# Partial sums of two recurrences formed by TensorE up to step 12 instead of step 7, with new instruction orders

## The chip, the cores and the metric

The kernel runs on one NeuronCore of one Trainium2 chip. The metric is the device time of one execution in microseconds, the median of several executions. A core has five engines with a queue each: TensorE (PE, with its weight loads as PEld), VectorE (DVE), ScalarE (ACT), GpSimd (POOL) and SyncE (SP). SP only issues DMAs here. The engines work through their queues strictly in the order written, and wait for each other at semaphores.

## The reference: what is computed

Two kinds of layer alternate, A, B, A, B, each with a layer norm before it and its result added to x (2048 tokens of 448 numbers).

```python
def _A_ref(x, mem0, Wq, Wk, Wv, Wo, seg_len):      # 16 heads of 256, 8 memory rows, segments of 32
    ...
    for s in range(n_seg):                          # 64 segments, one after the other
        h = jnp.concatenate([mem, xs], axis=1)      # 8 memory rows + 32 rows of x
        q, k, v = ...                               # h times Wq, Wk, Wv
        scores = jnp.einsum('bhqe,bhke->bhqk', q, k) * scale
        p = _softmax(jnp.where(mask, scores, -1e9))
        o = jnp.einsum('bhte,hed->btd', jnp.einsum('bhqk,bhke->bhqe', p, v), Wo)
        mem = o[:, :M, :].copy()                    # the next segment's memory
        outs.append(o[:, M:, :])
```

Layer B is a gated product: relu(x Wg) * (x Wu), times Wd. What makes it hard is `mem`: the 8 memory rows of segment s+1 are made from segment s, so layer A is a recurrence of 64 steps, and there are two of them (the first and the third layer). Only the 8 memory rows have to go through the recurrence. The other rows of a segment can be computed later, in tiles of 128 tokens.

## The kernel before, in words

**Folded weights.** At the start, Wq and Wk are folded into one matrix per head (tile `A`) and Wv and Wo into another (tile `Bsb`), so that scores are (h A) h^T and the output is P h Bsb.

**Steps.** The function `chain(step)` advances both recurrences by one segment. The second runs `LAG` = 7 steps behind the first. So steps 0 to 6 hold one recurrence, steps 7 to 62 both, and steps 63 to 69 the second alone. Columns 0 to 7 of the transposed memory `mT` belong to the first, 8 to 15 to the second. From step 7 on columns 16 to 31 carry 16 **riders**: rows of already finished tokens that are not part of a recurrence (their attention is computed along with it). One step is, on TensorE:

1. `U`, line 1268: mT times A, 112 matmuls into four banks, copied to `Usb` by ACT and DVE (line 1274).
2. Line 1444: turns `Usb` into `uTm`; then the scores, line 1467; softmax on DVE and ACT (lines 1477 to 1484); line 1507 turns the probabilities; line 1537 and 1541 multiply with the rows `HR`; the result is copied to `YTm`.
3. The **product**, line 1307: `YTm` times `Bsb`, 56 chunks. TensorE works on four column groups at once, so that the result lies in four partial sums in partitions 0-31, 32-63, 64-95 and 96-127 of one bank, and has to be added across partitions.
4. The **sum** of the four, and its transposition into the new `mT` by the column matmuls (line 1334 or 1350), which the next step's `U` needs.

The sum is made in one of two ways.

- Steps 0 to 6 (`step < LAG`, line 1312): the product is made in two halves of 256 and 192 columns. ACT copies each half of the bank as bf16 into `Hi` (line 1314), DVE writes bank minus Hi into `Lo` (line 1315), and eight column matmuls (line 1334, two for each of four blocks) with the selection matrix `Sel16` add the four parts, Hi and Lo, and transpose in one go. Two further matmuls (line 1341, the **row matmuls**) form the sum untransposed in 16 partitions, and a copy puts it into `Ohi` (line 1355).
- Steps 7 and later: ACT copies part 0 (line 1322), DVE adds parts 1, 2 and 3 one after the other (1324 twice, 1325) into `Ohi`, GpSimd or DVE doubles a piece (`twice`, line 1205), and four column matmuls (line 1350) transpose. In step 7 this is done in two halves (`step < SPLIT`), from step 8 on at once.

From `Ohi`, four DMAs write the new memory rows into `HR` (lines 1364 and 1365), and two more bring riders' rows to `Tsb` (line 1371).

**Where Hi and Lo lie.** They share their memory with `UR`. The riders' part of `Usb` is turned by DMA into `UR`, first for half v = 0, then for v = 1 (`turn_riders`, line 1415), and copied from there to `uTr` by ACT or DVE after each. The riders' scores (1467), softmax (1493 to 1501) and products (1534) run beside the chain.

**What fills the time between.** TensorE has other work: tiles of the attention (1626, 1655, 1537, 1693), of the gated product (1715, 1733) and norms (1580). A tile of the first layer becomes ready every four steps; those of the third layer start in step 15.

**Order.** Nothing is scheduled on the chip. The program lists some 9,300 operations, and `ORDER` says in which order and on which engine each is issued: an entry is 5 x operation + engine. `BANKS` gives the PSUM bank of each result. Both were found by a search outside the kernel. `FILLS` puts idle-running matmuls on zeros (line 183, tile `warm`) ahead of entries of `ORDER`: position, then how many, bank and shape.

Of the kernel before, what the change touches and what calls it, by code (L numbers as in the profile page):

```python
# [11 lines left out]
D = 448  # L12
# [272 lines left out]
def bass_interleave_layers__memory_aug_recurrent_mem_tr__glu_gated_reglu__prompt_kernel(  # L285
# [20 lines left out]
LAG = 7  # L306
# [1554 lines left out]
```

## Time and profile before

| what | us |
|---|---|
| median of 3 runs (1509.76 to 1510.58) | 1510.49 |
| the profiled execution | 1517.04 |
| its span on the core | 1515.3 |

The page of the profile gives each engine's busy share, then the chain of waits that ended last. The timeline lists instructions in order of time: start, duration, engine, line, tiles, how many; in brackets the idle time before it and what ended that. Durations of matmuls hold a constant tail: a matmul of 16 columns shows 0.169 us, one of 128 shows 0.217, one of 448 shows 0.353, and matmuls in a row start far closer together than that. So a wait of TensorE is about 0.17 us longer than the idle time shown. Steps, by the first matmul of line 1268 in each:

| step | starts at, us | length | warm matmuls in it | TensorE not busy |
|---|---|---|---|---|
| 7 | 170.6 | 16.3 | 0 | 0.85 |
| 8 | 186.9 | 18.2 | 0 | 1.59 |
| 9 | 205.1 | 16.6 | 7 | 0.63 |
| 10 | 221.7 | 16.0 | 46 | 0.66 |
| 11 | 237.7 | 18.8 | 0 | 1.00 |
| 12 | 256.5 | 16.9 | 0 | 0.45 |
| 13 | 273.4 | 20.9 | 0 | 2.31 |
| 14 | 294.3 | 20.7 | 0 | 2.98 |
| 15 | 315.0 | 19.0 | 0 | 0.04 |

### The profile page before, as it was taken

How to read it: one execution, taken by the hardware profiler on the slowest of the kernel's cores; microseconds unless marked ns; L12 is line 12 of the kernel's file. 1: busy time of each engine (PE TensorE's matmuls, PEld its weight loads, DVE VectorE, ACT ScalarE, POOL GpSimd, SP SyncE). 2: the span in 40 equal slices, each digit the busy share in tenths (PEclk: the TensorE clock that was granted, in tenths of full speed). 3: DMA queues.
4: the chain of work that ended last, by engine and by line, in shares of the span. 5: the costliest groups of instructions: out<-in, count | busy, mean ns of one | idle time of the engine just before them, and what ended most of it. 6: DMA issues, size and time to landing. Idle time of an engine off the chain costs nothing.

```text
span 1515.3 us, 83381 instructions
## 1 busy us (share of the span) xinstructions
PE 1478.4 (98%) x37579; PEld 1063.1 (70%) x37579; DVE 1109.6 (73%) x3353; ACT 841.0 (56%) x2383; POOL 60.0 (4%) x240
## 2 busy tenths in 40 slices
PE   8999999999999999999999999999999999999998
PEld 6576766667667776677767777677767676677675
DVE  7655768678776878678776778778777878778774
ACT  6755556556565556555655655555555556545542
POOL 1000000000000000000000000000000000000000
PEclk9999999999999999999999999999999999999999
DMA  9831122222222212212122223213222222213211
GB/s 237 194 89 44 28 43 44 44 37 46 46 39 41 45 32 51 42 31 52 44 42 38 44 44 53 40 35 47 47 44 31 52 43 53 39 41 40 47 27 27
DMA packets 239346, 78.20 MB, mean 52 GB/s; under 512 B 212104, under 2 KB 238992, under 8 KB 238992
## 3 DMA queue, kind: packets, MB, share of 16 engines
q1 hardware_dynamic: 238352, 72.60, 25.2%
q8 instruction: 297, 4.87, 1.4%
q14 instruction: 57, 0.47, 0.1%
q10 hardware_dynamic: 640, 0.26, 0.1%
HBM read 17.68 MB, written 1.84 MB: 13 GB/s over the span
## 4 chain that ended last, share of the span: by engine, by line
PE 87%; DVE 6%; DMA 3%; ACT 2%; issue 1%; SPq 1%; DVEq 0%; POOL 0%
PE psG L1626 14%; PE psG L1693 14%; PE psG L1715 11%; PE psC L1307 11%; PE psC L1268 7%; PE psG L1733 6%; PE psG L1268 5%; PE psG L1104 3%; PE psG L1537 2%; PE psG L1655 2%; PE psC L1467 1%; PE psC L1693 1%; PE psC L1444 1%; DMA UR<-Usb 1%; PE psC L1534 1%
## 5 line engine op out<-in xcount | busy, mean ns | idle before, releaser
L1693 PE MATMUL psG<-Bsb,YT 128*128 128x448 bf16 x1232 | 263.8, 353 | 0.0
L278 ACT ACTIVATE Ug<-psG 64x128 bf16<-64x128 f32 (+2 forms) x424 | 152.7, 374 | 73.6 <-PE psG L1626 64.5
L1307 PE MATMUL psC<-Bsb,YTm 128*32 128x448 bf16 (+2 forms) x4088 | 188.0, 335 | 1.0 <-DVE YTm L281 0.5
L1715 PE MATMUL psG<-G,glu 64*128 64x128 bf16 x5866 | 183.6, 216 | 2.6 <-DMA G<-xn 2.4
L1715 PEld LDWEIGHTS psG<-G,glu 64*128 64x128 bf16 x5866 | 170.3, 94 | 14.5 <-issue 8.6
L1626 PE MATMUL psG<-HT,A 64*128 64x128 bf16 x3424 | 175.8, 217 | 0.3 <-ACT Bsb L278 0.3
L1693 PEld LDWEIGHTS psG<-Bsb,YT 128*128 128x128 bf16 x1232 | 107.3, 97 | 89.0 <-issue 7.7
L1268 PE MATMUL psG<-A,mT 64*32 64x448 bf16 x4564 | 158.8, 350 | 2.8 <-issue 1.9
L1626 PE MATMUL psG<-HX,A 64*128 64x128 bf16 x2568 | 149.9, 217 | 0.0
L1307 PEld LDWEIGHTS psC<-Bsb,YTm 128*32 128x32 bf16 x4088 | 101.4, 97 | 67.2 <-DVE YTm L281 3.2
L281 DVE CAST Ug<-psG 64x128 bf16<-64x128 f32 (+2 forms) x277 | 114.9, 427 | 25.3 <-PE psG L1626 21.3
L1268 PE MATMUL psC<-A,mT 64*32 64x448 bf16 x3276 | 128.8, 351 | 1.0 <-issue 0.6
L1626 PEld LDWEIGHTS psG<-HT,A 64*128 64x128 bf16 x3424 | 116.6, 94 | 8.9 <-issue 5.0
L1324 DVE TENSOR_TENSOR Usb<-psC,Usb 32x448 f32<-32x448 f32 (+2 forms) x122 | 74.4, 610 | 63.7 <-ACT Usb L1322 60.9
L278 ACT ACTIVATE YT<-psG 128x448 bf16<-128x448 f32 x217 | 109.3, 538 | 20.3 <-PE psG L1541 20.0
L281 DVE CAST YT<-psG 128x448 bf16<-128x448 f32 x145 | 88.2, 618 | 41.2 <-PE psG L1541 40.4
L1720 ACT ACTIVATE hG<-psG 128x512 bf16<-128x512 f32 (+1 forms) x123 | 66.7, 543 | 81.6 <-PE psG L1715 78.8
L1268 PEld LDWEIGHTS psG<-A,mT 64*32 64x32 bf16 x4564 | 80.5, 92 | 32.3 <-issue 4.0
L1733 PE MATMUL psG<-glu,hG 128*128 128x448 bf16 x448 | 99.8, 353 | 0.0
L1268 PEld LDWEIGHTS psC<-A,mT 64*32 64x32 bf16 x3276 | 64.9, 93 | 45.4 <-ACT mT L278 2.7
L1626 PEld LDWEIGHTS psG<-HX,A 64*128 64x128 bf16 x2568 | 95.2, 94 | 0.0
L1626 PE MATMUL psG<-l,A 64*128 64x128 bf16 x2807 | 94.4, 216 | 0.0
(274 smaller groups left out, 2755.7 us busy)
## 6 DMA issues: line engine op xcount, KB each, us to landing
Bsb<-in_A_Wq_dram SPq DMA_DIRECT2D x6, 384.0 KB
Bsb<-in_A_Wk_dram SPq DMA_DIRECT2D x6, 384.0 KB
Tsb<-Ohi SPq DMA_DIRECT2D x128, 7.0 KB
UR<-Usb SPq DMA_TRANSPOSE x124, 2.9
X<-in_A_x_dram SPq DMA_DIRECT2D x16, 112.0 KB, 5.6
glu<-in_A_Wo_dram SPq DMA_DIRECT2D x4, 448.0 KB
out_dram<-X SPq DMA_DIRECT2D x16, 112.0 KB
glu<-in_B_W_gate_dram SPq DMA_DIRECT2D x14, 112.0 KB
```

Of the source, the lines that this page charges most:

```text
L278: return E.activation(out, i, ACT.Copy, scale=1.0 if scale is None else scale)
L281: return E.tensor_copy(out, i)
L1104: i = E.matmul(bk.ap()[row0:row0 + mn, 0:D], lhsT=lhs[:, et, m0:m0 + mn], rhs=rhs[:, et, :], start=(et == 0), stop=(et == 1), tile_positio ...
L1268: i = E.matmul(ub[v].ap()[32 * j:32 * j + 32, 0:D], lhsT=self.mT[rw, b, :], rhs=self.A[rw, b, a0:a0 + D], start=(b == 0), stop=(b == 6), t ...
L1307: x = E.matmul(bo.ap()[32 * j:32 * j + 32, 0:d1 - d0], lhsT=self.YTm[:, q, :], rhs=self.Bsb[:, chunks[q], d0:d1], start=(i == 0), stop=(i ...
L1324: s.add("dve", dv_cost(n), lambda E, e, j=j, a_=a_, part=part: E.tensor_tensor(a_, part(j), a_, ALU.add), r=[bo], w=w, part=(j, 0), **P)
L1537: return E.matmul(ps[:, n * q:n * q + n], lhsT=HR[rows, KM + 128 * q:KM + 128 * q + 128], rhs=PT, start=True, stop=True, tile_position=(b, 0))
L1626: i = E.matmul(ub[v].ap()[:, 128 * n:128 * n + 128], lhsT=self.A[rw, b, a0:a0 + 128], rhs=HT[rw, b, :, 0:SEG] if b < 4 else HX[rw, b - 4, ...
L1693: i = E.matmul(bo.ap()[:, 0:D], lhsT=YT[:, c, :], rhs=self.Bsb[:, 14 * g + c, :], start=(g == 0 and c == 0), stop=(g == 3 and c == 13))
L1715: i_ = E.matmul(two[v].ap()[:, 128 * c:128 * c + 128], lhsT=self.Wgu[rw, b, f0:f0 + 128], rhs=G[rw, b, :], start=(b == 0), stop=(b == 6), ...
L1720: s.add("act", 169 + 0.84 * N, lambda E, e, dst=dst, z=two[0], N=N: E.activation(dst, z.ap()[:, 0:N], ACT.Relu), r=[two[0]], w=[("hG", i, ...
L1733: i_ = E.matmul(bk.ap()[:, 0:D], lhsT=hG[:, c, :], rhs=self.Wd[:, c, :], start=(c == 0), stop=(c == NFC - 1))
```

## The change: what it does

Steps 7 to 11 form the sum the way steps 0 to 6 do (`FAST` = 12). The product is made in two halves there (`SPLIT` = 12). The row matmuls now give 32 rows in these steps, the riders' 16 among them, with a wider selection matrix `Sel32`, and `Ohi` is filled from them. The first copies into Hi and Lo of these steps wait until the riders' pieces of `UR` have been copied out, and the riders' DMA into `UR` waits until the matmuls of the step before have read Hi and Lo. `ORDER`, `BANKS` and `FILLS` are new.

```diff
-FILLS = {56: (11, 0, 0), 69: (9, 0, 0), 1306: (7, 2, 0), 1461: (46, 1, 1)}
+FILLS = {56: (11, 0, 0), 69: (9, 0, 0), 1116: (9, 0, 0), 1303: (8, 4, 0), 1418: (15, 0, 0), 1466: (19, 2, 1), 1775: (27, 1, 0), 1931: (11, 2, 0)}
...
-SPLIT = 8
+SPLIT = 12
+FAST = 12
...
-        self.Sel16 = sb("Sel16", [128, 16])
+        self.Sel32 = sb("Sel32", [128, 32])
+        self.Sel16 = self.Sel32[:, 0:16]
...
-        self.s.alias["UR"] = [(k, d) for k in ("Hi", "Lo") for d in (0, 256)] + ["Hi2", "Lo2"]
...
-        dve(lambda E: E.tensor_reduce(fv[:, 0:16].rearrange("p (c m) -> p c m", c=2),
-                                      fv[:, 64:128].rearrange("p (c j m) -> p c m j", c=2, j=4), AX.X, ALU.add),
-            r=["cf2"], w=["cf"])
-        dve(lambda E: E.tensor_copy(self.Sel16[:, :], fv[:, 0:16]), r=["cf"], w=["Sel16"])
+        dve(lambda E: E.tensor_reduce(fv[:, 0:32], self.ident.rearrange("p (j q) -> p q j", j=4), AX.X, ALU.add), r=["ident", "cf2"], w=["cf"])
+        dve(lambda E: E.tensor_copy(self.Sel32[:, :], fv[:, 0:32]), r=["cf"], w=["Sel16"])
...
+        ur = ["UR"] if LAG <= step < FAST else []
         for d0, d1 in ((0, 256), (256, D)) if step < SPLIT else ((0, D),):
...
-            if step < LAG:
+            if step < FAST:
                 hi, lo = (z[:, 64 + d0:64 + d1] for z in self.HL)
-                s.add("act", 169 + 0.84 * n, ..., r=[bo], w=[("Hi", d0)], **P)
+                s.add("act", 169 + 0.84 * n, ..., r=[bo], w=[("Hi", d0)] + ur, **P)
-                s.add("dve", dv_cost(n), ..., r=[bo, ("Hi", d0)], w=[("Lo", d0)], **P)
+                s.add("dve", dv_cost(n), ..., r=[bo, ("Hi", d0)], w=[("Lo", d0)] + ur, **P)
...
-        if step < LAG:
+        if step < FAST:
             for ks, r in ...
+            nr = 16 if step < LAG else 32
             def rows(E, e):
                 for z in range(2):
-                    i = E.matmul(br.ap()[0:16, 0:D], lhsT=self.Sel16[:, :], ...)
+                    i = E.matmul(br.ap()[0:nr, 0:D], lhsT=self.Sel32[:, 0:nr], ...)
...
-        if step < LAG:
-            s.add(EV, ev_cost(D), copy_any(O[0:16, 64:XW], lambda: br.ap()[0:16, 0:D]), ...)
+        if step < FAST:
+            s.add(EV, ev_cost(D), copy_any(O[0:nr, 64:XW], lambda: br.ap()[0:nr, 0:D]), ...)
...
-        self.turn_dma(self.UR[:, 0:7, :], ..., w=["UR"], **P)
+        self.turn_dma(self.UR[:, 0:7, :], ..., w=["UR"] + [(k, d) for k in ("Hi", "Lo") for d in (0, 256)] + ["Hi2", "Lo2"], **P)
```

The two long lists read, once each entry is divided by 5 and the operation looked up, as follows. Three more operations a step are issued in steps 8 to 11 (12 in all; in step 7 the number stays the same). By the start of step 12 TensorE has issued the same other work in both lists, and again by the starts of steps 13 and 17; from step 27 on its order is the same to the end, and ACT's and DVE's differ in a few entries. What TensorE issues between the last product matmul of a step and the first column matmul, that is, while the sum is formed:

| step | list before | list after |
|---|---|---|
| 7 | 10 of line 1693 | 5 of line 1693 |
| 8 | 56 of 1626, riders' scores | nothing |
| 9 | 56 of 1626, 84 of 1715 | riders' scores |
| 10 | 46 warm | 19 warm |
| 11 | 56 of 1626, 5 of 1693, 40 of 1537/1541, 16 of 1655 | 5 of 1693, the row matmuls of step 10 |
| 12 | 19 of 1693, 20 of 1537/1541 | the same |
| 13 | 112 of 1715 | 42 of 1626, 84 of 1715 |
| 14 | 42 of 1626 | 112 of 1626 |

Elsewhere: in step 6 the list after puts a pair of row matmuls (line 1341) among the matmuls of line 1444 and 56 of line 1626 behind them, where the list before has nothing and the norm's four matmuls (1580). In the wait for the softmax (between 1467 and 1507) the list after has 5 of line 1693 and 9 warm matmuls in step 7, 4 of line 1733 and 15 warm ones in step 10, and in step 13 only 27 warm ones where the list before has 56 of line 1626 and the riders' products. Step 13 has 4.3 us less of other TensorE work in the list after, step 14 4.0 us more (112 of 1715 stand behind its `U`), and 11 warm matmuls stand behind step 14's column matmuls. On SP, the four DMAs into `HR` of steps 7, 8 and 9 are issued behind the next step's first riders' DMA instead of ahead of it, so between the riders' two DMAs.

More of the change, by code (lines that the diff above doesn't have):

```diff
@@ L1311, in chain @@
             part = lambda j, bo=bo, n=n: bo.ap()[32 * j:32 * j + 32, 0:n]
-            if step < LAG:
+            if step < FAST:
                 hi, lo = (z[:, 64 + d0:64 + d1] for z in self.HL)
-                s.add("act", 169 + 0.84 * n, lambda E, e, hi=hi, bo=bo, n=n: E.activation(hi, bo.ap()[:, 0:n], ACT.Copy), r=[bo], w=[("Hi", d0)], **P)
+                s.add("act", 169 + 0.84 * n, lambda E, e, hi=hi, bo=bo, n=n: E.activation(hi, bo.ap()[:, 0:n], ACT.Copy), r=[bo], w=[("Hi", d0)] + ur, **P)
                 s.add("dve", dv_cost(n), lambda E, e, hi=hi, lo=lo, bo=bo, n=n: E.tensor_tensor(lo, bo.ap()[:, 0:n], hi, ALU.subtract),
-                      r=[bo, ("Hi", d0)], w=[("Lo", d0)], **P)
+                      r=[bo, ("Hi", d0)], w=[("Lo", d0)] + ur, **P)
                 if d0 == 0:
@@ L1337, in chain @@
             br = self.bank("C", "G")
+            nr = 16 if step < LAG else 32
             def rows(E, e):
                 for z in range(2):
-                    i = E.matmul(br.ap()[0:16, 0:D], lhsT=self.Sel16[:, :], rhs=self.HL[z][:, 64:XW], start=(z == 0), stop=(z == 1), tile_position=(0, 0))
+                    i = E.matmul(br.ap()[0:nr, 0:D], lhsT=self.Sel32[:, 0:nr], rhs=self.HL[z][:, 64:XW], start=(z == 0), stop=(z == 1), tile_position=(0, 0))
                 return i
@@ L1353, in chain @@
         self.halves(self.mT[:, :, 0:16], pk, 16, bc_, "mTm", ("mTh",), P=P)
-        if step < LAG:
-            s.add(EV, ev_cost(D), copy_any(O[0:16, 64:XW], lambda: br.ap()[0:16, 0:D]), r=[br], w=["Ohi", ("Ohi", 256)], **P)
+        if step < FAST:
+            s.add(EV, ev_cost(D), copy_any(O[0:nr, 64:XW], lambda: br.ap()[0:nr, 0:D]), r=[br], w=["Ohi", ("Ohi", 256)], **P)
         for c, sg, _ in act:
@@ L1414, in turn_riders @@
         s, P = self.s, dict(prio=0.5)
-        self.turn_dma(self.UR[:, 0:7, :], self.Usb[:, 896 * v:896 * v + 896], 240000, r=[("Usb", 2 * hh + v) for hh in range(2)], w=["UR"], **P)
+        self.turn_dma(self.UR[:, 0:7, :], self.Usb[:, 896 * v:896 * v + 896], 240000, r=[("Usb", 2 * hh + v) for hh in range(2)], w=["UR"] + [(k, d) for k in ("Hi", "Lo") for d in (0, 256)] + ["Hi2", "Lo2"], **P)
         R = self.UR.rearrange("p (h k) (j q) -> p h k j q", h=2, j=4)
```

838 rows, old and new, of tables (BANKS, ORDER) are left out of this document.

## The prediction

> **What bounds the kernel now.** I read the page first, its busy shares and the chain of waits that ended last.
>
> ```profile
> PE 1478.4 (98%) x37579; PEld 1063.1 (70%) x37579; DVE 1109.6 (73%) x3353; ACT 841.0 (56%) x2383; POOL 60.0 (4%) x240
> ...
> PE 87%; DVE 6%; DMA 3%; ACT 2%; issue 1%; SPq 1%; DVEq 0%; POOL 0%
> ```
>
> TensorE is the bound: 98% busy, 87% of the chain. So added matmuls cost time, except where TensorE stands idle anyway. Where that is, the table of busy times by stretch tells; here are steps 10, 13, 14 and 15, and then seven us inside step 14 (stretch, its length, PE, PEld, DVE, ACT, POOL busy with counts, granted clock).
>
> ```profile
> 221.70:237.70 16.00, 15.34 (x369) 10.79 (x370) 11.75 (x40) 8.93 (x31) 0.73 (x3) 1.00 0.21 49
> ...
> 273.40:294.30 20.90, 18.59 (x554) 14.46 (x554) 14.22 (x45) 9.62 (x27) 0.96 (x4) 1.00 0.26 43
> 294.30:315.00 20.70, 17.72 (x403) 12.17 (x399) 14.61 (x49) 9.89 (x31) 0.50 (x2) 0.86 0.15 34
> 315.00:334.00 19.00, 18.96 (x506) 13.54 (x502) 14.97 (x42) 11.71 (x36) 0.50 (x2) 0.98 0.31 41
> ...
> 309.00:316.00 7.00, 6.37 (x128) 5.44 (x136) 4.45 (x20) 3.32 (x11) 0.50 (x2) 0.51 0.08 20
> ```
>
> From step 15 on TensorE is full (18.96 of 19.00). Before that it is not, and step 14 has the clock halved besides. As the other work issued is the same in both lists by the starts of steps 12, 13 and 17, a microsecond gained or lost before step 15 should reach the end. The third view is the timeline of one slow sum, step 10's.
>
> ```profile
> 231.42 1.24 SPq L1046 DMA_TRANSPOSE UR<-Usb  x1
> ...
> 234.12 2.73 PE L183 MATMUL psC<-warm 128*32 128x128 bf16 x46
> ...
> 234.34 0.53 ACT L1322 ACTIVATE Usb<-psC 32x448 f32<-32x448 f32 x1
> 234.91 1.27 DVE L1324 TENSOR_TENSOR Usb<-psC,Usb 32x448 f32<-32x448 f32 x2 [1.21 <-ACT Usb L1322]
> 235.57 0.52 ACT L278 ACTIVATE uTr<-UR 128x384 bf16<-128x384 bf16 x1 [0.70 <-DMA UR<-Usb]
> 236.21 0.62 DVE L1325 TENSOR_TENSOR Ohi<-psC,Usb 32x448 bf16<-32x448 f32 x1
> ...
> 237.11 0.26 PE L1350 MATMUL psC<-Sel,Ohi 128*128 128x16 bf16 x4 [0.26 <-DVE Ohi L1205]
> ```
>
> The product's last matmul gives way to warm ones at 234.12, and the column matmuls start at 237.11: a slow sum takes 3.0 us, all of it idle running here. The fast form, step 1:
>
> ```profile
> 86.61 0.40 PE L1626 MATMUL psG<-HT,A 64*128 64x128 bf16 x8
> 86.72 0.33 ACT L1314 ACTIVATE UR<-psC 128x192 bf16<-128x192 f32 x1 [0.77 <-PE psC L1307]
> ...
> 87.09 0.36 DVE L1315 TENSOR_TENSOR UR<-psC,UR 128x192 bf16<-128x192 f32 x1 [0.46 <-ACT UR L1314]
> ...
> 87.50 0.36 PE L1334 MATMUL psC<-Sel,UR 128*128 128x16 bf16 x8
> 87.78 0.55 PE L1341 MATMUL psC<-UR,Sel 128*16 128x448 bf16 x2
> ```
>
> From the first matmul behind the product (86.61) to the columns (87.50) is 0.9 us; from the product's own end I take 1.0. Last, the two large stalls of steps 13 and 14:
>
> ```profile
> 289.04 3.30 PE L1715 MATMUL psG<-G,glu 64*128 64x128 bf16 x112 [2.24 <-DMA G<-xn]
> ```
>
> ```profile
> 309.08 0.27 PE L1350 MATMUL psC<-Sel,Ohi 64*128 64x16 bf16 x4 [1.99 <-DVE Ohi L1205]
> ```
>
> **The change part by part**, against the profiled execution's span of 1515.3 us (1517.04 with what lies around it, 6.55 above the median of the timed runs; the median gets the same difference).
>
> Matmuls added. The row matmuls take 0.55 - 0.17 of tail = 0.38 us. Eight column matmuls show 0.36 where four show 0.26: 0.10. The product in two halves (step 7, 112 matmuls shown as 2.87) against whole (56 shown as 2.83): 0.04. Five steps of 0.48 and four of 0.04 make **+2.5 us**. Bounds: +0.6 if all row matmuls lie where TensorE would stand, +2.5 if none does.
>
> The sums of steps 7 to 11. Before, TensorE loses in step 7 0.4 (0.24 shown before line 1350, and the tail), in step 8 1.4 (0.48 and 0.58 shown, two tails), in step 10 3.0 (warm ones included), in 9 and 11 some 0.1 each, as 3.9 us of tile work cover them: 5.0 us. After, a sum needs 1.0. The list covers it with 0.95 in step 7 (5 of line 1693), nothing in 8, 0.2 in 9, warm ones alone in 10, 1.3 in 11. Lost: 0.05 + 1.0 + 0.8 + 1.0 + 0 = 2.9. Difference **-2.1**; bounds -5.0 and 0. The DVE adds that go (three of 0.62 a step) and the Lo copies that come were no bound (DVE 73%).
>
> The rest of steps 7 to 11. The tile work that covered the slow sums covers other waits now, but partly where nothing waits: step 7's softmax has 0.95 us of cover where step 14's shows 1.75 to be needed, step 10's 0.76. I lay those 1.8 us of new waits against the ones before that a DMA made: line 1537 for HR 0.62, line 1534 for Tr 0.78, each with a tail, 1.7 together, which may well stay away in a new order. **0**, bounds -2 and +2.
>
> The riders' DMAs, a wait added on ACT and DVE. Hi may be written only when the second riders' piece has left UR. In step 10 that DMA is issued at 231.42 and ACT, which waited for it, reads at 235.57: 4.15 us; two with a copy of 0.5 us after each need 9.3. From the end of the Usb copies to the product's end the timeline gives 9.7, 10.8, 8.4, 8.8 and 9.75 us in steps 7 to 11. So there is hardly room. Queued behind a waiting Hi on ACT are the mT copies, behind a waiting Lo on DVE the riders' softmax. In step 8 SP now has four HR DMAs of 0.65 (lines 1364, 1365), one of HR<-xn and the riders' Pr (1.2) between the two: the second is issued 7.1 us after the first at the least, 11.8 until it is copied, 1.0 more than the 10.8. In 9 and 10 six DMAs (3.9 us) stand there, about as long as the first riders' DMA is under way. **+1.0**; bounds 0 (all hidden) and +9.9 (2.6 us of HR DMAs added whole to 9.3, against the room above in steps 8 to 11: 1.1 + 3.5 + 3.1 + 2.2). The HR rows themselves land some 6 us later than before, 9 to 10 us into a step, just as line 1537 needs them: inside these bounds.
>
> Steps 3 to 6. In step 6 TensorE waits 0.19 and 0.22 before line 1444 and 0.23 before 1467, 1.15 with tails; row matmuls and tile work stand there now. **-0.9**, bounds -1.15 and 0.
>
> Steps 13 and 14. The sum's wait in step 14 goes, as 112 matmuls of line 1626 (3.1 us) cover it: -2.2. With it should go the halved clock (0.51 from 309 to 316: 6.8 us, of which 1.0 waiting; half of 5.8 is 2.9): -2.9. New: step 13's softmax has 27 warm matmuls for cover, +1.75, and 11 more, +0.6. The stall at line 1715 stays: both lists put its first matmul some 8.1 us after line 1693's last of the tile, and the G transposes landed 10.5 after. Sum **-2.7**; bounds -4.9 (that stall goes too) and +0.2 (the clock is halved all the same).
>
> Steps 15 to 69: **0**, bounds -1 and +1: TensorE's order is the same from step 27, and before that its fill is moved by fractions of a us. The selection matrix at the start: two DVE instructions for two, hidden behind the loading of weights, 0.
>
> Sum: 2.5 - 2.1 + 0 + 1.0 - 0.9 - 2.7 + 0 = **-2.2 us**: span 1513.1, median **1508.3**, 0.15% faster.
>
> **What the skill would make of it.** The profile showed the clock halved after one stall of 2.0 us (step 14) and whole after one of 2.2 (step 13). The Trainium skill, TensorE: Matmul & The Clock Gate, section "What's actually happening", asks for an idle window of about 3.4 us, in windows that run free of the kernel. The first half this trace contradicts; the second fits that two equal stalls end differently. Second, the row matmuls use a slice of the array (128*16) that their neighbours do not: in step 1 they start 0.28 after the eight column matmuls began, with no idle time shown around them. The Trainium skill, TensorEngine Tiling (Array Packing), section "Key Properties", says that each change of tiling mode drains TensorE: at a tail of 0.17 for two changes in five steps that would be +1.7, and the sum -0.5. The trace shows no such gap, so I leave it out.
>
> **The rivals.**
>
> *The waits on DMAs go.* The new order avoids both the G stall (-2.4) and the 1.7 us of steps 7 and 11, and the riders' DMAs are hidden (-1.0): -7.3, median 1503.2. For it: those were waits for single DMAs, and any other order meets them otherwise. Against: SP issues nearly without pause from 269 to 285, 0.6 to 1.3 us each, and nothing in the change takes DMAs away.
>
> *The riders' DMAs set the step.* If the second one is issued more than some 5 us after the first, Hi waits, and the whole chain of the step with it, in steps 8 to 11: +9.9 instead of +1.0, median 1517.2. For it: the room measured above is 8.4 to 10.8 against a need of 9.3. Against: SP's HR DMAs fit into the time that the first riders' DMA needs anyway.
>
> *The clock.* A stall of 2.2 us remains in step 13 and one of 1.0 with little around it in step 8; one halving costs 2.9: 1511.2. The same comes out if the timed runs of before never had the halving that the profile shows. With a second halving, 1514.1, slower.
>
> *The sum's time does not count*: what the sums no longer wait for, other links of the chain wait for, and the stalls of steps 13 and 14 only move; +2.5 of matmuls and +1.0 of riders' DMAs against nothing gained, 1514.0.
>
> **How the numbers follow.** 0.2% is 3.0 us and about what a measurement can tell from no change: faster is below 1507.5, slower above 1513.5. My forecast with the one-halving clock case: 0.37. DMA waits go: 0.35. Riders' DMAs 0.14, two halvings or a sum that does not count 0.14, together slower 0.28. The likeliest case's own range is 1507.5 to 1513.5. The bounds added up run from 1497 to 1526; leaving out some 2 in 10 gives 1501 (below the fast rival) to 1518 (above the slow one).
>
> **What would show it.** Right: line 1315 and 1334 in steps 7 to 11, 1.0 us from product to columns, TensorE's waits before line 1350 gone there; step 12 starting within 1 us of 256.5; clock 1.00 through step 14; step 15 some 2 us earlier than 315.0, and the same lead at the end. Wrong: ACT at line 1314 waiting for a copy out of UR in steps 8 to 11 (the slow side), line 1715 in step 13 without its wait for G (the fast side), a halved clock at another place, or a lead at step 15 that shrinks behind it.

## The result, and the profile after

The kernel after takes 1521.43 us (median of four, 1520.15 to 1525.53), the kernel before 1510.47 (four runs, 1509.76 to 1510.58): 11.0 us slower. The ratio, taken over all runs, is 1.0078, 95% interval 1.0058 to 1.0099, that is 11.8 us (8.8 to 15.0). The forecast was 1508.3, with 1501 to 1518 as range. The profiled execution of after took 1522.55 us (span 1520.7) against 1517.04 (1515.3): there the gap is 5.5 us, half of the timed one. After's profiled execution is one of its four timed ones; that of before is none of its four and lies 6.5 us above them.

The page of after, busy shares and the chain that ended last:

```profile
PE 1484.0 (98%) x37869; PEld 1072.6 (71%) x37869; DVE 1112.3 (73%) x3372; ACT 837.3 (55%) x2368; POOL 60.8 (4%) x242
...
PE 78%; DVE 4%; DMA 2%; ACT 1%; SPq 1%; issue 1%
```

TensorE is still the bound, busy for 5.6 us more. In the code of after the lines have moved: the product's sum is lines 1314 to 1343, the y products 1536 and 1539, G's products 1717, transposing DMAs 1045. The busy times by stretch of after (stretch, length, PE, PEld, DVE, ACT, POOL busy with counts, granted clock), steps 10, 11, 13, 14, 15 and 56, and 6.8 us inside step 56:

```profile
223.80:240.70 16.90, 16.66 (x453) 12.49 (x453) 10.90 (x34) 9.03 (x31) 0.73 (x3) 1.00 0.21 45
240.70:261.90 21.20, 19.38 (x596) 15.30 (x596) 17.24 (x60) 13.18 (x38) 1.00 (x4) 1.00 0.28 41
278.40:294.60 16.20, 15.79 (x427) 11.60 (x427) 12.06 (x39) 9.13 (x30) 0.50 (x2) 1.00 0.26 53
294.60:315.60 21.00, 20.37 (x563) 14.90 (x560) 16.43 (x55) 9.66 (x24) 0.73 (x3) 1.00 0.16 33
315.60:336.00 20.40, 19.64 (x555) 14.58 (x553) 16.87 (x52) 12.81 (x38) 0.50 (x2) 1.00 0.23 41
1192.90:1223.40 30.50, 25.34 (x633) 19.10 (x630) 19.28 (x61) 14.60 (x44) 0.97 (x4) 0.89 0.26 43
1209.20:1216.00 6.80, 4.52 (x84) 4.06 (x88) 1.96 (x5) 1.95 (x4) 0.00 (x0) 0.50 0.25 53
```

The last column but two is the granted clock. A stretch in which it is 0.50 is called a halving below, and a wait of TensorE a stall. The halving of step 14 is gone (1.00) and one stands in step 56. From the first matmul of U of each step, the start of a step in after less that in before: 0.7 at step 0, -0.5 at step 7, +5.4 at step 12, +5.0 at 13, +0.3 at 14, +0.5 at 15, -1.2 at 56, +5.6 at 57, +5.5 at 69. So the profile has three places: steps 7 to 11 lose 5.9, steps 12 to 14 win 4.8 back, and step 56 alone loses 6.85 (30.44 us against 23.59). Step 56 of after, the lines of SP's transposes and of their users. `Px` is the softmax of a tile of the attention; a DMA turns it into `Tx`, which TensorE multiplies with. `G` is turned from `xn` for the gated product, and `UR` belongs to the riders:

```profile
1202.32 2.57 SPq L1045 DMA_TRANSPOSE G<-xn  x2
...
1203.30 0.33 DVE L1670 TENSOR_TENSOR Px<-Tx,stx 128x160 bf16<-128x160 f32 x1
...
1204.99 2.78 SPq L1045 DMA_TRANSPOSE UR<-Usb  x1
1207.80 2.54 SPq L1045 DMA_TRANSPOSE Tx<-Px  x2
...
1211.48 0.50 PE L1539 MATMUL psG<-Tx,l 40*128 40x128 bf16 x6 [4.54 <-DMA Tx<-Px]
```

Px is written by 1203.63, but its transpose is issued behind two G and the riders' second UR transpose, and lands at 1211.5; TensorE has nothing else and waits 4.7 us (4.54 in the bracket, a tail more). In before, one Tx transpose goes ahead of G and the other ahead of UR:

```profile
1203.66 1.24 SPq L1046 DMA_TRANSPOSE Tx<-Px  x1
...
1204.95 1.26 SPq L1046 DMA_TRANSPOSE G<-xn  x1
...
1206.26 1.89 SPq L1046 DMA_TRANSPOSE Tx<-Px  x1
1207.23 0.21 PEld L1537 LDWEIGHTS psG<-Tx,l 40*128 40x128 bf16 x6
1207.29 0.33 PE L1537 MATMUL psG<-Tx,l 40*128 40x128 bf16 x6
```

TensorE's order is the same in both; the orders of SP (seven transposes), ACT and DVE differ in steps 53 to 59.

### The profile page after: what moved, and what is told of

Same layout as the page of the kernel before. It is cut to its first block, busy times and chain, and to the rows that moved or that the text cites. A ratio compares the mean times of both kernels' runs of the same rounds, so it can differ in the third digit from the quotient of the medians.

```text
span 1520.7 us, 83982 instructions
## 1 busy us (share of the span) xinstructions
PE 1484.0 (98%) x37869; PEld 1072.6 (71%) x37869; DVE 1112.3 (73%) x3372; ACT 837.3 (55%) x2368; POOL 60.8 (4%) x242
## 4 chain that ended last, share of the span: by engine, by line
PE 78%; DVE 4%; DMA 2%; ACT 1%; SPq 1%; issue 1%
PE psG L1628 14%; PE psG L1695 13%; PE psG L1717 11%; PE psC L1307 10%; PE psC L1267 6%; PE psG L1735 5%; PE psG L1267 4%; PE psG L1539 2%; PE psG L1657 2%; PE psC L1469 1%; DMA UR<-Usb 1%; PE psC L1446 1%; PE psC L1536 1%; PE psG L1307 1%; PE psC L1695 1%; PE psG L1543 1%
## 5 line engine op out<-in xcount | busy, mean ns | idle before, releaser
L1695 PE MATMUL psG<-Bsb,YT 128*128 128x448 bf16 x1288 | 276.1, 353 | 0.1
L1695 PEld LDWEIGHTS psG<-Bsb,YT 128*128 128x128 bf16 x1288 | 112.0, 97 | 93.7 <-issue 8.4
L1307 PEld LDWEIGHTS psC<-Bsb,YTm 128*32 128x32 bf16 x4256 | 105.1, 97 | 63.6 <-DVE YTm L281 3.9
L281 DVE CAST Ug<-psG 64x128 bf16<-64x128 f32 (+2 forms) x291 | 120.1, 425 | 26.4 <-PE psG L1628 21.7
L1324 DVE TENSOR_TENSOR Usb<-psC,Usb 32x448 f32<-32x448 f32 x110 | 67.9, 617 | 56.0 <-ACT Usb L1322 53.4
```

Source lines behind the costliest of these rows:

```text
L281: return E.tensor_copy(out, i)
L1307: x = E.matmul(bo.ap()[32 * j:32 * j + 32, 0:d1 - d0], lhsT=self.YTm[:, q, :], rhs=self.Bsb[:, chunks[q], d0:d1], start=(i == 0), stop=(i ...
L1324: s.add("dve", dv_cost(n), lambda E, e, j=j, a_=a_, part=part: E.tensor_tensor(a_, part(j), a_, ALU.add), r=[bo], w=w, part=(j, 0), **P)
L1695: i = E.matmul(bo.ap()[:, 0:D], lhsT=YT[:, c, :], rhs=self.Bsb[:, 14 * g + c, :], start=(g == 0 and c == 0), stop=(g == 3 and c == 13))
```

## The experiments

All differences are worked out from such ratios to the kernel before, timed on the same chip (its medians there: 1510.5 on the first, 1516 to 1519 on the others, where its executions lie between 1511 and 1526). By medians some come out otherwise: e2 at +8.0, e10 at +13.5. In brackets the 95% interval, in us. Lengths of steps are from the one profile of each run.

| run | what it is | against before, us | step 11 | step 56 |
|---|---|---|---|---|
| before, after | first chip | after +11.8 (8.8 to 15.0) | 18.8, 21.2 | 23.6, 30.4 |
| e1 | after, steps 53-59 old | +6.2 (3.8 to 8.7) | 24.8 | 23.6 |
| e2 | before, steps 53-59 new | +6.7 (4.3 to 9.1) | 19.2 | 31.6 |
| e3 | new to step 12 | +8.4 (6.2 to 10.3) | 24.5 | 24.2 |
| e4 | new to step 14 | +6.8 (4.4 to 9.3) | 24.6 | 23.8 |
| e5 | after again | +11.2 (7.6 to 14.9) | 23.2 | 29.3 |
| e6 | after, SP order of steps 11, 56 | +10.5 (8.2 to 12.7) | 20.0 | 29.5 |
| e7 | before with new sums, behind UR's copies | +19.4 (16.2 to 22.8) | 22.9 | 24.1 |
| e8 | after, warm in step 56 | +12.9 (10.5 to 15.3) | 23.0 | 29.5 |
| e9 | before with new sums, Hi and Lo in uTm | +8.9 (5.6 to 12.4) | 20.3 | 23.2 |
| e10 | after, Hi and Lo in uTm | +16.7 (12.9 to 20.3) | 20.1 | 30.8 |
| e11 | e10, steps 11 and 53-59 mended | +6.2 (3.8 to 8.6) | 20.3 | 23.3 |
| e12 | before again, one profile | | 19.1 | 23.5 |
| e13 | before, warm in step 14 | -1.5 (-3.5 to +0.6) | 19.2 | 24.2 |
| e14 | before, steps 13-14 new | -1.1 (-3.6 to +1.4) | 18.9 | 22.9 |
| e15 | e1, SP of step 56 new, one profile | | 20.8 | 29.0 |
| e16 | e9, ACT's queue mended, 13-14 new | +4.4 (2.4 to 6.5) | 22.0 | 23.8 |

### Which stretch loses: e1 to e5

The order is a list of entries; at the cuts used here both lists have issued the same work, so that stretches can be exchanged.

```diff
 e1, in after:
-    entries 7416 to 7574 (steps 53 to 59) and their banks
+    entries 7404 to 7562 of before
 e2, in before: the exchange the other way
 e3, e4: after up to step 12 or 14, then the entries of before
```

> The kernel after, with the order's entries of steps 53 to 59 (159 of 9307, and their banks) put back as in the kernel before; everything else as after. Theory A (the late stretch: in step 56 SP issues two Tx transposes behind a G and a UR transpose, TensorE stands 4.7 us and the clock halves): step 56 takes about 23.5 us again instead of 30.4, the lead of the profile falls from +5.5 to about -1, and the timed difference to before falls from +11 by 6 to 7, to some +4. Theory B (the timed kernel loses in steps 7 to 14, where the profiled run of before had 6.5 us more than its timed runs): it falls by less than 3, the clock halves somewhere else or the stall only moves, and +8 to +11 stays.

> The kernel before, with only the entries of steps 53 to 59 taken from the kernel after. Theory A: +6 to +7 us against before, with TensorE's stall of 4 to 5 us ahead of the Tx,l products of step 56 and a halved clock behind it. Theory B: 0 to +3, the stall depends on what runs ahead of it.

> The kernel after up to step 12 (the new sums, and the new orders of steps 2 to 12), and from step 13 on the order of the kernel before, without the two rows of warm matmuls of steps 13 and 14. By the traces, step 13 starts 5.0 us later than before. Theory A: +5 (+4 to +6), as what is lost before step 13 reaches the end; step 14's halved clock as in the profile of before. If the profile of before had 6.5 us that its timed runs lack in these steps: +8 to +12. If the tail makes up for it: 0 to +2.

> The kernel after up to the end of step 14 (with its warm matmuls there, the last row of them into another bank), and from step 15 on the order of the kernel before. By the traces, step 15 starts 0.5 us later than before. Theory A: 0 to +1.5, that is 4 to 5 less than the kernel that is new only up to step 12. Theory B, that timed runs of before do not have the halved clock of step 14: +3 to +6, hardly less than the kernel new to step 12.

> The kernel after as it is, beside the other three on the same chip. If the two losses add up (early stretch +6.5 and late stretch +6.7, each against before on another chip): +11 to +13 against before. If the late loss shrinks where the early one is there: +7 to +9.

The late stretch alone costs +6.7 (e2). With it, or with half of it (e6, e15, below), step 56 takes 29.0 to 31.6 us in seven profiles, without it 22.9 to 24.2 in the eleven others, both of before's among them. Theory A is right there, but not in the early half: e3 and e4 are slower than the first profiles made expect (+5 and 0 to +1.5). What is new up to step 12 costs +8.4, steps 13 and 14 give back 1.6 of it at best guess, which the intervals can't tell from nothing, and e1, free of the late loss, stays at +6.2, where some +4 was expected. Early 8.4, less 1.6, and late 6.7 add up to 13.5; measured are +11.8 and +11.2, within the intervals.

The early loss is larger than the first profile says. In the seven profiles with after's orders untouched there (after, e1, e3, e4, e5, e8, e15), steps 7 to 11 take 5.9 to 10.2 us more than in the first profile of before, 8.4 in the mean; in the four others with before's orders (e2, e12, e13, e14) they stay within 0.4 of it. Step 11 is part of that. The timeline of e1:

```profile
254.62 0.19 PE L1543 MATMUL psG<-PTm,l 40*128 40x64 bf16 x1
256.57 0.51 PE L1539 MATMUL psC<-Tx,HR 40*128 40x128 bf16 x6 [1.76 <-DMA Tx<-Px]
```

And the busy times of the 6.8 us that follow in e1, with the clock at 0.50:

```profile
255.60:262.40 6.80, 5.83 (x124) 5.06 (x128) 3.64 (x12) 2.12 (x6) 0.50 (x2) 0.50 0.08 17
```

TensorE waits 1.8 us for a Tx transpose that stands behind others on SP, and the clock is halved; e3 and e4 show the same after waits of 1.5, e5 and e8 a halving of 3.4 us after 1.4 and 1.5. In the first profile of after this wait was 1.1 us, in e15 under 0.5, and the clock held. Step 11 takes 23.0 to 24.8 us with the halving and 21.2 and 20.8 without.

e1's profile as a whole says nothing of its gain: it is the second slowest of nine executions and ends 12.6 us behind the first profile of before. 5.5 us of that come between steps 43 and 54, a stretch that comes back under e11.

### SP's queue, and the queues behind it: e6, e15, e8

```diff
 e6, SP's order in step 56
-  G, G, UR<-Usb, Tx<-Px, Tx<-Px, G, G
+  Tx<-Px, G, Tx<-Px, UR<-Usb, G, G, G
 and in step 11
-  Tsb<-Ohi x2, UR<-Usb, Tx<-Px, Tr<-Pr, Tx<-Px
+  UR<-Usb, Tx<-Px, Tr<-Pr, Tx<-Px, Tsb<-Ohi x2
 e15: e1, with the upper order ("-") in step 56 alone
 e8, in after:
-FILLS = {..., 1931: (11, 2, 0)}
+FILLS = {..., 1931: (11, 2, 0), 7563: (76, 0, 0)}
```

> The kernel after with SP's order alone changed, at two places: in step 56 its seven transposes in the order of the kernel before (a Tx first, the other Tx ahead of UR), in step 11 the two Tsb DMAs of 1.29 us together moved behind the second Tx transpose. TensorE's, ACT's and DVE's orders stay. Theory (transposes queued on SP make both stalls): step 56 30.4 to some 23.6, step 11 21.1 to 19.9 (from 24.8 where the clock halves there), 8 to 11 us less than after. Rival (the stalls of TensorE move to the transposes and DMAs that come later now): 0 to 4 less.

> The kernel after with the entries of steps 53 to 59 as in before, but SP's seven transposes of step 56 in the order of after: so SP's order is new, TensorE's, ACT's and DVE's are old. With the run that had SP's order old and the others new this makes four corners. If SP's order alone makes the stall: step 56 takes 28 to 31 us, TensorE waiting for Tx. If it takes the new ACT and DVE orders too: 23 to 25 us.

> The kernel after with 76 warm matmuls (4.2 us at full clock) ahead of the products of Tx and l of step 56, where TensorE waits 4.7 us for the Tx transposes; nothing else is changed. If an idle TensorE is what halves the clock: no halved clock near 1209, step 56 some 2.3 to 3.4 us shorter (27 to 28), the wait for the transposes stays. If the halving does not come from the idle time: step 56 stays at 30.4 or grows.

In step 11, e6 does what was expected: 20.0 us, no halved clock. In step 56 the rival came true. The timeline of e6:

```profile
1212.31 0.33 PE L1539 MATMUL psG<-Tx,l 40*128 40x128 bf16 x6
...
1212.49 1.24 SPq L1045 DMA_TRANSPOSE UR<-Usb  x1
...
1217.25 0.52 ACT L278 ACTIVATE uTr<-UR 128x384 bf16<-128x384 bf16 x1 [3.91 <-DMA UR<-Usb]
...
1218.24 0.54 ACT L278 ACTIVATE YTm<-psC 128x448 bf16<-128x448 f32 x1
...
1218.92 4.19 PE L1307 MATMUL psC<-Bsb,YTm 128*32 128x448 bf16 x56 [3.54 <-DVE YTm L281]
```

The products of Tx no longer wait (1212.31). But UR is transposed later now, and in after's orders of ACT and DVE the copies out of UR stand ahead of the copies into YTm: both engines wait 3.7 to 3.9 us for UR, YTm stands behind them, and TensorE waits 3.7 us for YTm. With the orders the other way about (e15: SP new, ACT and DVE old) the first stall is back: 3.85 us, step 56 29.0. So either half of the new orders alone makes a stall of about the same size (one profile each), and they don't add.

e8 parts the stall from the clock:

```profile
1215.51 4.42 PE L183 MATMUL psC<-warm 128*128 128x128 bf16 x76
1221.06 0.34 PE L1539 MATMUL psG<-Tx,l 40*128 40x128 bf16 x6 [1.13 <-DMA Tx<-Px]
```

The clock stays at 1.00 through the step, where all six other profiles with a stall here have a halving (3.4 or 6.8 us). From the first product of Tx to the step's end it takes 9.8 us, against 11.9 in after: a halving costs some 2.1. But the step is no shorter, since the transposes landed 1.1 us later in it (the two Tx issues took 3.33 us together, 2.54 in after). It was expected to take 27 to 28 us and takes 29.5, and the kernel isn't faster timed.

### The new sums alone: e7, e9, e10, e16

```diff
 e7: the code of after; each new sum near the place of the old one, but on ACT and DVE behind the
     riders' copies out of UR; all else ordered as in before
-FILLS = {56: (11, 0, 0), 69: (9, 0, 0), 1306: (7, 2, 0), 1461: (46, 1, 1)}
+FILLS = {56: (11, 0, 0), 69: (9, 0, 0)}
 e9 (e7) and e10 (after), steps 7 to 11:
-  HL = the two halves of UR;  Hi, Lo: w=[("Hi", d0)] + ["UR"]
+  HL = the two halves of uTm; Hi, Lo: w=[("Hi", d0)], after=[readers of uTm]
 and in e9 alone: Hi and Lo on ACT and DVE in the old sum's places, ahead of the riders' copies
 e16: e9, Hi's and Lo's second half right behind the product on ACT and DVE; steps 13 and 14 of after
```

> The kernel before with the new sums alone in steps 7 to 11: every other instruction in the order of before on its engine (three entries of ACT apart), the 53 warm matmuls of steps 9 and 10 left out. By my terms: matmuls +2.5, TensorE's losses at the sums (5.0) gone, since the work that covered the slow sums now stands ahead of the column matmuls, riders' DMAs +1.0: -1.5 against before. Rival 1 (the riders' DMAs set the step, as Hi waits for the second copy out of UR): +5 to +10, with ACT waiting for UR at line 1314. Rival 2 (the sums' form is free, and the new orders alone cost): -3 to 0, and step 13 starts no later than in before.

> The kernel before with the new sums in steps 7 to 11, as the kernel that was 18 us slower, but Hi and Lo of these steps stand in the memory of uTm, which lies unused between a step's scores and the next step's copies, and no longer in that of UR. So Hi no longer waits for the riders' second transpose and its copies; every other instruction stands in the order of the kernel before. Theory (the wait for UR was the cost of the sums): no ACT or POOL instruction of the sums waits for uTr any more, step 13 starts within 2 us of the kernel before instead of 14.8 later, -2 to +2 against before. Rival (the row matmuls, the added DMAs' waits or the halved clock were the cost): step 13 still starts 8 us or more later, +8 to +18.

> The kernel after, its orders untouched, with Hi and Lo of steps 7 to 11 in the memory of uTm, so that the wait for the riders' second transpose is taken away and nothing else. Theory (the orders of after already hide that wait, 1.2 us of it shows on ACT): 0 to 1.5 us less than after, +9 to +11 against before. Rival (the wait still sets the steps 7 to 11): 4 us or more less than after, step 13 starting near before's.

> The kernel before with the new sums of steps 7 to 11 in the memory of uTm, the order otherwise old, Hi's and Lo's second half now first in ACT's and DVE's queues behind the product (in step 10 it stood behind another tile's norm and TensorE waited 2.2 us), and the order of steps 13 and 14 from after. If the sums' waits were what still cost there: 2 to 4 us less than the run with the sums in their own place (+8.9), and with steps 13 and 14 (-1) +3 to +6 against before, step 13 starting 1 to 2.5 later than in before. If it beats before, the new sums can pay: below 0.

e7 is the slowest of all, with step 13 starting 14.8 us later than in before. Its step 10:

```profile
238.98 2.87 PE L1307 MATMUL psC<-Bsb,YTm 128*32 128x256 bf16 x112
...
239.25 1.36 SPq L1045 DMA_TRANSPOSE UR<-Usb  x1
...
243.80 0.52 ACT L278 ACTIVATE uTr<-UR 128x384 bf16<-128x384 bf16 x1 [2.02 <-DMA UR<-Usb]
...
244.40 0.38 ACT L1314 ACTIVATE UR<-psC 128x256 bf16<-128x256 f32 x1
...
245.51 0.27 PE L1334 MATMUL psG<-Sel,UR 128*128 128x16 bf16 x4 [3.67 <-DVE UR L1204]
```

The product is done at 241.85, but the copy into Hi (line 1314) starts at 244.40, behind the copy out of UR of a transpose that was issued at 239.25, and the column matmuls wait 3.7 us. e9 takes away what makes it wait: Hi and Lo lie in other memory, and so may stand ahead of the copies out of UR on ACT and DVE. Both together give 10.5 us back (on another chip; in the profiles step 13 starts 10.6 us earlier). So rival 1 of e7's expectation holds in its mechanism: the riders' DMAs set the step. Its price of +5 to +10 was too low; e7 is at +19.4, and its profile has halvings of 3.4 and 6.8 us behind the stalls of steps 9 and 10, where e9 has one of 3.4. In after's order new memory alone changes little in the profile, as was expected (e10: step 13 starts 1.3 us earlier than in the first profile of after). Its timed +16.7 lies above after's +11.2, though the intervals overlap, and nothing in its profile explains it. e11, which has the same memory, is no slower than e1, which hasn't.

e9 is still 8.9 us slower than before, where -2 to +2 was expected, and its step 13 starts 4.2 us later. In its step 10 Hi's second half stands on ACT behind the norm of another tile and TensorE waits 2.2 us (then 3.4 us of halved clock). e16 mends that (step 10 takes 15.6 us, not 17.1) and takes steps 13 and 14 from after: +4.4. But its profile doesn't show that the mend gained anything: step 11 takes 22.0 us instead of 20.3, with a halving of 3.4 us at its start and a wait of 1.05 us for Tr where e9 waits 0.2, and step 13 starts 4.3 us later than in before, not the 1 to 2.5 expected. No arrangement tried makes the new sums pay.

### Steps 13 and 14, and the clock in before: e12 to e14

```diff
 e13, in before:
+FILLS: 1906: (32, 0, 0)      (ahead of the column matmuls of step 14)
 e14, in before:
-    entries 1742 to 1916 (steps 13 and 14)
+    those of after, with its 27 warm matmuls
```

> The kernel before as it is, profiled a second time on another chip. If the halved clock of step 14 is not what this kernel usually does: clock 1.00 through step 14, which takes some 17.3 us and not 20.75, and what lies behind it within a few us of the first profile. If it always does: the clock halves near 309 again.

> The kernel before with 32 warm matmuls (1.8 us) ahead of the column matmuls of step 14, where its profile shows a stall of 2.0 us and the halved clock behind it. If timed runs mostly lack that halving (their granted clocks are 0.998 to 1.000): -1 to +1 against before. If they have it as the profile does: -2.5 to -3.5.

> The kernel before with the order of steps 13 and 14 alone taken from after (175 entries, with the 27 warm matmuls of step 13). By the two profiles these steps are 4.5 us shorter. If timed runs of before have the halved clock of step 14: -4 to -5 against before. If they lack it: 3.4 less of that, 0 to -1.5, the G stall of step 13 (2.4) being gone and other waits in its place.

The busy times of steps 13 and 14 of e12:

```profile
273.50:294.10 20.60, 18.60 (x558) 14.49 (x559) 14.19 (x45) 9.59 (x27) 0.96 (x4) 1.00 0.24 44
294.10:314.00 19.90, 16.86 (x402) 11.36 (x400) 14.59 (x49) 9.87 (x31) 0.50 (x2) 0.91 0.15 34
```

And of step 13 of e13, whose order there is the same:

```profile
273.30:291.90 18.60, 18.52 (x554) 14.47 (x554) 13.92 (x44) 9.72 (x27) 0.97 (x4) 1.00 0.34 48
```

A G stall of 2.1 us is in e12 and not in e13 (18.60 long, 18.52 busy); the halving of step 14 lasts 6.8 us in the first profile, 3.4 in e12, and after the same stall of 2.16 us in e9 there is none. That e12 would have none was the expectation, and it was wrong. Of 80 executions of before beside these runs, 71 have a granted clock of 0.998 or more, where the first profile has 0.997 and e12, with its short halving, 0.998. So part of the gain of steps 13 and 14 is a gain against a long first profile: against e2 and e12, which have before's order there too, after's two steps are 3.2 and 3.3 us shorter, not 4.5. Timed, their new order is worth -1.1 (-3.6 to +1.4), and e13, whose clock stays at 1.00, -1.5 (-3.5 to +0.6); neither can be told from nothing, nor e14 from the 3.3 of the profiles. e13 is a weak test: its warm matmuls waited 1.9 us themselves and ran behind the stall, so that they added their 1.8 us.

### All mended: e11

```diff
 e10, with e1's steps 53 to 59 and e6's step 11
```

> The kernel after with Hi and Lo in the memory of uTm, the entries of steps 53 to 59 as in before, and the two Tsb DMAs of step 11 behind the second Tx transpose. If the losses found add up: step 56 23.6 us, step 11 about 20, +1 to +3 against before (+11 less 6.5, 1.2 to 3, and 0 to 1.5). If something in the new order of steps 13 to 52 costs besides: +4 to +7.

Each mended place is right (step 11 20.3, step 56 23.3), and still +6.2. Step 15 starts 2.5 us before that of the first profile of before, but step 6 did already by 2.0, ahead of the new sums; steps 7 to 11 cost 5.5 us here too. Between steps 43 and 54, where its order is that of before but for a few entries of ACT and DVE, this profile loses 6.5 us against the first one of before. But with before's order there e12 loses none, e3 0.5, e13 3.1, e9 3.8 and e4 5.0. So most of such a loss can come without any change of order, and whether the few entries add to it isn't settled; the last section has what the traces show.

## Why the prediction was wrong

**Steps 15 to 69: 0, bounds -1 and +1.** This step failed: +5 in the profile, step 56 alone +6.85, and +6.7 (4.3 to 9.1) timed. "TensorE's order is the same from step 27" was true and not enough: a stall was made without one entry of TensorE moving. SP's late order was to be had and was not compared, and the few entries of ACT and DVE that were seen to differ were put at nothing. None of the rivals had it either.

It wasn't the only step to fail. The terms up to step 12 (the next two paragraphs, and steps 3 to 6) come to +0.5; e3 times what is new up to step 12 at +8.4 (6.2 to 10.3). With the late loss alone the forecast would have come to 1515.0, with the early one alone to 1516.2, both inside the range of 1501 to 1518; together they lead out of it. Of the signs named, step 12 was to start within 1 us of 256.5 and starts 5.4 later, and a halved clock at another place came, in step 56.

**Matmuls added: +2.5.** Measured some +3.5: TensorE's time in steps 7 to 11 less its idle time is 77.7 us against 74.3, with two warm matmuls (0.1) fewer. The idle time hangs on the tail that is taken off, so this is good to some 0.3. Half of the excess is in the row matmuls. In after, step 8:

```profile
190.26 0.35 PE L1267 MATMUL psG<-A,mT 64*32 64x448 bf16 x1
190.42 0.35 PE L1267 MATMUL psC<-A,mT 64*32 64x448 bf16 x1
...
190.44 0.35 PE L1267 MATMUL psG<-A,mT 64*32 64x448 bf16 x1
190.72 0.55 PE L1343 MATMUL psC<-UR,Sel 128*32 128x448 bf16 x2
191.21 0.27 PE L1469 MATMUL psG<-l,uTr 128*128 128x40 bf16 x4
```

And in before, where no row matmuls stand there:

```profile
189.46 0.35 PE L1268 MATMUL psG<-A,mT 64*32 64x448 bf16 x1
189.74 0.37 PE L1467 MATMUL psC<-l,uTr 128*128 128x40 bf16 x8
```

From U's last matmul to the riders' first it takes 0.76 us in after (0.77 by the rounded starts) and 0.28 in before, so the two row matmuls take 0.48, not 0.38: 0.10 more, 0.5 in five steps. Two matmuls of 448 columns of one form follow each other in 0.19 us, the other form begins after 0.28. The Trainium skill, TensorEngine Tiling (Array Packing), section "Key Properties", says that a change of tiling mode drains TensorE. The trace agrees, at some 0.09 us for a change; the row matmuls add one change a step, as there is one without them, and not two. I left it out for want of a gap in the trace: TensorE shows as busy throughout. The other 0.5 us has no term that the runs show.

**The sums of steps 7 to 11: -2.1, the rest of these steps: 0, the riders' DMAs: +1.0.** Forecast -1.1, measured +2.5 in TensorE's idle time (11.5 before, 14.0 after; a tail of 0.16 is taken off each matmul). The sums do get shorter: from the product's end to the first column matmul the five steps take 4.1 us instead of 16.0. But the work that stood there stands ahead of the product now: from U's start to the product's it is 67.8 us instead of 51.6. On an engine that is busy, a shorter wait is worth only the idle time that it held, and other waits lost the work that had covered them. That is the rival "the sum's time does not count" in its mechanism; its price, +3.5 for matmuls and riders' DMAs, was too low, as it counted no new waits and no halving.

The riders' DMAs as a rival had the right mechanism, but not for the kernel after: e7 against e9 shows 10.5 us for it. That this is near my upper bound of 9.9 is partly luck, as the bound counted waits alone and the 10.5 hold halvings too. In after's order Hi waits only 1.2 us for the copies out of UR in all five steps, because the product starts 1.7 to 4.7 us later in each. Whether the search put it later for that reason is argued, not shown.

**Steps 3 to 6: -0.9.** -1.2 between the two profiles. That pair proves little: e2, with before's order there, has -1.2 as well. In the mean the ten profiles with after's order are 1.0 us shorter there than the eight with before's. Right, as far as that shows.

**Steps 13 and 14: -2.7.** In the profile -4.5: the halved clock went, as said, and so did the stall at line 1715, which I had kept; step 13 is 16.2 us long. Timed it is -1.1 at best guess (-3.6 to +1.4, which holds the forecast too). What failed is the sentence "the median gets the same difference": the profiles differ by 5.5 us and the medians by 11.0. That before's timed runs mostly have neither loss in full would explain part of it; their clocks agree with that, but they have no trace.

**The rivals.** The fast one, "the waits on DMAs go", was right for the G stall and wrong in that waits for DMAs went elsewhere: to the Tx transposes of steps 11 and 56. "The clock" was right in kind: one halving in step 56, and in step 11 in five of the seven profiles with after's orders untouched there. Its place followed from SP's queue, which no rival looked at in these steps.

What stays open: how the timed gap on the first chip comes to 11 where the two profiles there give 5.5. The halving (2.1 to 2.9) and the G stall (2.1 to 2.4) of before's profile, both shown to come and go, would make most of it, but the timed runs have no trace. Nor is it on record on which chip the first profile of before was taken; 1517.04 is an ordinary time for this kernel on the other chips. And e10's time stays open.

## What to carry to other kernels

Where an order is searched anew, compare every queue's order over the whole kernel, not only the bounding engine's: here 159 late entries that touch none of the new sums cost about as much as all the rest. One profile of each kernel isn't enough for a difference of some us: the same order gave 0 to 5 us in one stretch. When a wait on a busy engine is removed, count the idle time inside it, not its length, and then find where its cover goes. A buffer lent to a second use is a wait on that buffer's queue; look for another that lies unused at that moment before ordering around it. With uTm that gave 10.5 us in the old order; in after's order it gave 1.3 us in one profile and nothing timed.

## What the hardware showed

- A stall and its halving don't go together one to one: stalls of 2.15 us ahead of step 14's column matmuls gave 6.8 (before), 3.4 (e2, e7, e12) or no us (e3, e9) of halved clock, and one of 1.8 us in step 11 gave 6.8 (e1). All halvings ahead of the last step last 3.4 or 6.8 us. The Trainium skill, TensorE: Matmul & The Clock Gate, section "What's actually happening", has a free-running window of 3.4 us, and lets the clock fall after an idle window of that length. The lengths and the chance agree with the window; that it takes so long an idle time, the traces contradict.
- SP's time to issue one transposing DMA is 1.25 us in the median, but in every profile 75 to 89 of the 354 such issues took over 1.5. Steps 44 of e3 and e4 have the same order and take 18.1 and 20.1 us: the first UR transpose took 1.24 us to issue in e3 and 2.01 in e4, the second landed 16.6 and 18.5 us into the step, and TensorE waits 1.6 us for the copy out of it in e4 alone. A chain that goes through a full SP queue is therefore not the same from run to run; that this is what e9 and e11 lost between steps 43 and 54 is likely, not shown.
